# Forty products of zeros among the first four pairs of an attention and two-layer MLP kernel

## The chip, the cores and the metric

The kernel runs on one core of one Trainium2 chip. The metric is the device time of one execution in microseconds (us); of several executions the median counts. Before the change, three runs gave 1048.25, 1048.41 and 1051.59 us, so the median is 1048.41 us.

## The reference, cut to what matters

Causal attention over 4 batches, 8 heads, 576 positions of 64 channels, mixed with a read of a memory matrix, then two dense layers with a gate between their matrices, one after the other.

```python
scores = scale * np.matmul(q, k.transpose(0, 1, 3, 2))       # causal mask, softmax -> a
local = np.matmul(a, v)
mem_out = einsum('bhsd,bhde->bhse', phi(q), M_prev) / (einsum('bhsd,bhd->bhs', phi(q), z_prev) + 1e-6)
x = g * mem_out + (1 - g) * local                             # (2304, 512)
h = x @ w_in;  x = (h * sigmoid(1.702 * h)) @ w_out           # d_ff 2048
h = x @ w_in2; x = (h * clip(h + 3, 0, 6) / 6) @ w_out2
```

## The kernel before

The 2304 rows of x are cut into six tiles of 384 (`TILES`, a tile is one (batch, block) segment of 384 positions or two segments of 192). Attention works on one *pair* at a time: two heads of one segment; pairs 0 to 3 make tile 0. The generator `attention` runs three stages of a pipeline over pairs: in step i `scores(i)` issues the score products of pair i, `turn(i - 1)` the transposes of the softmax of the pair before, and `weigh(i - 2)` the products with v. `mem_read(i - 1)` issues the products with the memory matrix. The engines share a pair's work like this:

- PE (TensorE): score products `s` (line 424, by the helper `mm`), transposes `t` (line 439, `at_transpose`), memory products `mem` (line 409, `at_matmul`), and `o`, the transposed memory part and the products with v (line 424 again).
- DVE (VectorE): mask and row minimum of `s` (line 484), sums and reciprocals of `st` (lines 492 and 493), scaling of `mem` (lines 676 to 680), and `phi` (lines 654 and 655).
- ACT (ScalarE): the exponential `p` (line 489), the copies `pt` of the transposes out of PSUM (line 584), the copy of `o` into x (line 736).
- POOL (GpSimd): the norm of `p` (line 497).

PSUM has eight banks. While tile 0 is made, `bank` hands out all eight in turn (`banks[0] = 8`), so a product into a bank waits until the reader of what stood there has read it. After tile 0 the attention of tile t + 1 is mixed into the first dense layer of tile t: `h` (lines 342, and 344 to 347) and `y` (lines 313, and 315 to 317). The first tile's `h` and `y` multiply in full fp32, the rest in fp32r. The weights are made on DVE and ACT (lines 186 to 206) before that.

A scheduler places the instructions of each engine into one fixed order when the program is built, so an edit at one place can move instructions of other engines. At run time each engine takes its queue strictly in that order.

At the very start a tile `warm` of zeros is set by DVE, and PE multiplies it nine times with itself into a bank that nobody reads (`WARM = 9`).

Of the kernel before, what the change touches and what calls it, by code (L numbers as in the profile page):

```python
# [9 lines left out]
F32R = mybir.dt.float32r  # L10
# [12 lines left out]
NT = 384  # L23
# [27 lines left out]
AB = None  # L51
LAG = 3
WARM = 9
AHEAD = 2
TWB = (3, 2)
EARLY = 3
# [20 lines left out]
def f32(ap):  # L77
    return ap.bitcast(F32)
# [26 lines left out]
def attention_moe_kernel(ctx: ExitStack, tc: tile.TileContext, qk0, sk0, sk1, vm0, vm1, bb, w1, w2, out):  # L105
    nc = tc.nc
    PE, ACT, DVE, POOL, SP = nc.tensor, nc.scalar, nc.vector, nc.gpsimd, nc.sync
# [4 lines left out]
    gp = ctx.enter_context(tc.tile_pool(name="gp", bufs=2))  # L112
# [38 lines left out]
    def load_w(n):  # L151


        while w_at[0] < min(n, len(w_jobs)):
            key = layer, f = w_jobs[w_at[0]]
            w_at[0] += 1
            pool, tag = slot(layer, f)
            w_raw[key] = pool.tile([128, 2, 2 * DM], I32, tag=tag, bufs=1, name=f"r{f}")
            for a in range(2):
                move(0, out=w_raw[key][:, a], in_=(w1, w2)[layer][f, a].bitcast(I32))  # L160
# [7 lines left out]
    def conv_w():  # L168
# [7 lines left out]
        if layer == 0:  # L176
            load_w(min(NF, w_at[1] + AHEAD))
        z = 2 if layer == 1 else int(f > PRE)
# [203 lines left out]
    def bank(name):  # L382
        k = banks[1] % banks[0]
        banks[1] += 1
        if k < 3:
            t = psa.tile([128, 512], F32, tag="a", bufs=3, name=name)
            at = ("a", banks[2] % 3)
            banks[2] += 1
        else:
            tag = ("h", "y0", "y1", "y2", "y3")[k - 3]  # L390
            t = psy.tile([128, 512], F32, tag=tag, name=name)
            at = (tag, 0)
        place[id(t)] = at, t
        return t
# [10 lines left out]
    on_pe = []  # L405
    marks = [None]

    def at_matmul(out, **args):
        on_pe[:] = [PE.matmul(out, **args).ins]  # L409
# [28 lines left out]
    def at_transpose(*args):  # L438
        on_pe[:] = [PE.transpose(*args).ins]  # L439

    def attention(ap):
# [7 lines left out]
        def start(key, gen):  # L449
            gens[key] = chains.start(after_gates(gen, AB))  # L450

        def need(*keys):
            for key in keys:
                gen = gens.pop(key, None)
                if gen is not None:
                    chains.finish(gen)
# [122 lines left out]
        def evac(i, jobs):  # L579

            yield
            for e, out, in_, *bank_done in jobs:
                if e is ACT:
                    d = ACT.copy(out=out, in_=in_)
                else:
                    d = DVE.tensor_copy(out=out, in_=in_)
                made.setdefault(i, {})[e] = d.ins
                for t in bank_done:
                    has_read(t, d)

        def turn(i):
            ti, si, b, g, p, _ = pairs[i]
            if g == 0:
                pt[i] = []
                for a in range(2):
                    t = ap.tile([128, 2 * N0], F32, tag="pt", bufs=PTB, name="pt")
                    pt[i].append(t)
                    need(("s", i, 0), ("s", i, 1))
                    s = pp[i][a]
                    for jj in range(2):  # L600
                        ps = bank("t")
                        src = (((0, 0), (0, 128), (1, 0)), ((0, 256), (1, 128), (1, 256)))[jj]
                        for x, (y, c) in enumerate(src):
                            at_transpose(ps[:, x * 128:(x + 1) * 128], s[y][:, c:c + 128], ident)
                        start(("t", i, a, jj), evac(i, [((ACT, DVE)[EV0[jj]], t[:, jj * 384:(jj + 1) * 384], ps[:, 0:384], ps)]))
                        yield
            else:
                pt[i] = []
                for a in range(2):
                    t = ap.tile([128, 4, N1], F32, tag="pt", bufs=PTB, name="pt")  # L610
                    pt[i].append(t)
                    need(("s", i, 0))
                    ps = bank("t")
                    for j in range(4):
                        at_transpose(ps[:, j * 128:(j + 1) * 128], pp[i][a][0][:, j * 128:(j + 1) * 128], ident)
                    start(
                        ("t", i, a, 0),
                        evac(i, [((ACT, DVE)[EV1[a]], t[:, :, 0:128], ps.rearrange("p (j c) -> p j c", j=4), ps)]),
                    )
                    yield  # L620
                need(("s", i, 2))
                s, s5 = pp[i][2]
                ps = bank("t4a")
                for j in range(3):
                    at_transpose(ps[:, j * 128:(j + 1) * 128], s[:, j * 128:(j + 1) * 128], ident)
                ps2 = bank("t4b")
                at_transpose(ps2[:, 0:128], s[:, 384:512], ident)
                at_transpose(ps2[0:64, 128:256], s5, ident)
                v = ps[:, 0:384].rearrange("p (j a c) -> p j a c", j=3, a=2)
                start(  # L630
                    ("t", i, 0, 1),
                    evac(
                        i, [((ACT, DVE)[EV1[2 + a]], pt[i][a][:, 0:3, 128:192], v[:, :, a], *(ps,) * a) for a in range(2)]
                        + [(DVE, pt[i][a][:, 3, 128:192], ps2[:, a * 64:(a + 1) * 64]) for a in range(2)]
                        + [(DVE, t4[0:64], ps2[0:64, 128:256].rearrange("p (a c) -> p a c", a=2), ps2)]
                    ),
                )
                yield
            pp.pop(i)
# [117 lines left out]
        for i in range(NPAIR + 2):  # L757
            if has(i):
                gs[i] = scores(i)
            if has(i - 1):  # L760
                gt[i - 1] = turn(i - 1)
            if has(i - 2):
                gw[i - 2] = weigh(i - 2)
            s, t, w = gs.pop(i, nil), gt.pop(i - 1, nil), gw.pop(i - 2, nil)
            for gen, n in (
                (s, 1), (t, 1), (w, 1), (s, 1), (t, 1), (w, 9), (s, 1), (t, 1), (s, 9),
            ):
                yield from chunks(gen, n)
            if has(i):
                start(("p", i), mem_prep(i))  # L770
                load_qk(i + 2)
            if has(i - 2) and pairs[i - 2][5]:
                need(("x", i - 2))
                yield pairs[i - 2][0]
            load_vm(i)
            if has(i - 1):
                yield from mem_read(i - 1)
            yield from chunks(t, 9)


    with ExitStack():
        warm = gp.tile([128, 2, NT], F32R, tag="g", bufs=2, name="warm")
        DVE.memset(f32(warm[:, 0]), 0.0)
        s = bank("warm")
        for _ in range(WARM):
            PE.matmul(s[:, 0:NT], lhsT=warm[:, 0, 0:128], rhs=warm[:, 0], start=True, stop=True)
        ident = const.tile([128, 128], F32, name="ident")
        make_identity(nc, ident)
        mask = const.tile([128, 512], F32, name="mask")
# [169 lines left out]
```

## Time and profile before

| | |
|---|---|
| median of 3 runs | 1048.41 us |
| span of the profiled execution, taken as its own time | 1049.0 us |
| PE busy | 1029.6 us (98%) |
| DVE, ACT, POOL busy | 467.4, 510.2, 293.7 us |
| mean granted TensorE clock | 0.995 |

The profile shows one execution on the core. The clock is given as a share of 2.4 GHz: 1.00 is 2.4 GHz and 0.50 is 1.2 GHz. A row of the order-of-time view gives the start, the time from the first start to the last end of a run of alike instructions, the engine, the line, the operation, and in brackets the idle time ahead of it and what ended that. Ends of PE's products are modelled, starts are not. A product with full fp32 operands on 64 rows or with a fp32 result of several passes can be two records, so counts in the trace can be twice those of the program. The profiled execution's span stands 0.6 us over the median of the runs.

### The profile page before, as it was taken

What the parts mean: (1) busy time and instruction counts of PE and PEld (TensorE: products, weight loads), DVE (VectorE), ACT (ScalarE), POOL (GpSimd) and SP (SyncE); (2) the same over time, 40 slices, a digit from 0 to 9 for tenths busy, and PEclk for the clock granted to TensorE, in tenths of its full rate; (3) what the DMA queues carried; (4) which work ended last, traced back from release to release, by engine and by line L of the source; (5) the groups of instructions that cost most, each with busy time, mean ns of one, the idle gap of its engine ahead of it and who ended that gap; (6) DMA issues with size and microseconds to landing.
All of it is one profiled execution on the core that took longest, in us unless ns stands there. A gap on an engine that the chain in (4) does not pass through costs nothing.

```text
span 1049.0 us, 16113 instructions
## 1 busy us (share of the span) xinstructions
PE 1029.6 (98%) x6025; PEld 914.9 (87%) x6025; DVE 467.4 (45%) x1153; ACT 510.2 (49%) x1110; POOL 293.7 (28%) x346
## 2 busy tenths in 40 slices
PE   8899999999999999999999999999999999999998
PEld 5555558988888888898889999999999999999998
DVE  6977766666533343433443697971121211211110
ACT  5876746545634454433333778883232332332322
POOL 4522112333333332322222241332222222222221
PEclk8999999999999999999999999999999999999999
DMA  5864314332211021111100784001010010000000
GB/s 185 277 232 137 136 55 153 129 118 65 81 42 36 26 67 46 31 31 61 47 16 16 271 302 173 18 11 52 1 46 16 10 52 1 31 31 1 31 1 30
DMA packets 33885, 80.27 MB, mean 77 GB/s; under 512 B 4112, under 2 KB 13328, under 8 KB 33808
## 3 DMA queue, kind: packets, MB, share of 16 engines
q1 hardware_dynamic: 33808, 79.25, 22.4%
q8 instruction: 47, 0.77, 0.3%
q14 instruction: 30, 0.25, 0.1%
HBM read 61.41 MB, written 9.44 MB: 68 GB/s over the span
## 4 chain that ended last, share of the span: by engine, by line
PE 86%; DVE 6%; ACT 5%; issue 2%; DMA 1%; SPq 0%; POOL 0%; DVEq 0%; ACTq 0%
PE y L315 11%; PE h L344 11%; PE y L317 11%; PE y L316 11%; PE h L347 11%; PE h L346 11%; PE s L424 5%; PE o L424 5%; PE h L342 3%; PE y L313 3%; PE t L439 3%; ACT p L489 2%; PE mem L409 1%; DVE s L484 1%; DVE r L191 1%
## 5 line engine op out<-in xcount | busy, mean ns | idle before, releaser
L295 POOL TENSOR_TENSOR g<-t,g 128x384 fp32r<-128x384 f32 x173 | 185.2, 1071 | 481.6 <-ACT g L292 433.0
L344 PE MATMUL h<-xs,w 128*128 128x384 f32 x704 | 241.4, 343 | 1.6 <-DVE t L283 0.9
L315 PE MATMUL y<-g,w 128*128 128x384 f32 x704 | 237.2, 337 | 0.5 <-ACT g L292 0.5
L316 PE MATMUL y<-g,w 128*128 128x384 f32 x704 | 236.3, 336 | 0.0
L346 PE MATMUL h<-xs,w 128*128 128x384 f32 x704 | 236.0, 335 | 0.3 <-DVE w L228 0.3
L347 PE MATMUL h<-xs,w 128*128 128x384 f32 x704 | 236.0, 336 | 0.0
L317 PE MATMUL y<-g,w 128*128 128x384 f32 x704 | 223.6, 338 | 0.0
L287 DVE SCALAR_TENSOR_TENSOR t<-t,h 128x384 f32<-128x384 f32 x96 | 53.0, 553 | 275.5 <-ACT t L285 275.4
L344 PEld LDWEIGHTS h<-xs,w 128*128 128x128 f32 x704 | 132.3, 188 | 10.1 <-issue 5.2
L285 ACT ACTIVATE t<-h,three 128x384 f32<-128x384 f32 x96 | 55.6, 580 | 170.2 <-PE h L347 170.1
L497 POOL TENSOR_SCALAR p<-p,st,omg 128x128 f32<-128x128 f32 (+3 forms) x128 | 85.8, 683 | 186.3 <-DVE st L493 122.1
L317 PEld LDWEIGHTS y<-g,w 128*128 128x128 f32 x704 | 130.4, 188 | 5.6 <-issue 4.9
L315 PEld LDWEIGHTS y<-g,w 128*128 128x128 f32 x704 | 132.2, 188 | 2.8 <-issue 1.3
L292 ACT CAST g<-t 128x384 fp32r<-128x384 f32 x176 | 90.1, 514 | 90.9 <-DVE t L287 49.3
L346 PEld LDWEIGHTS h<-xs,w 128*128 128x128 f32 x704 | 132.4, 188 | 0.7 <-DVE w L228 0.5
L316 PEld LDWEIGHTS y<-g,w 128*128 128x128 f32 x704 | 132.2, 188 | 0.7 <-issue 0.5
L347 PEld LDWEIGHTS h<-xs,w 128*128 128x128 f32 x704 | 132.2, 188 | 0.5 <-issue 0.5
L489 ACT ACTIVATE p<-s,st 128x512 f32<-128x512 f32 (+4 forms) x160 | 82.5, 524 | 73.3 <-DVE st L484 61.5
L484 DVE CUSTOM_DVE_ANT_0 s<-s,mask 128x128 f32<-128x128 f32 (+3 forms) x144 | 72.3, 529 | 72.1 <-PE s L424 71.3
L281 ACT ACTIVATE t<-h 128x384 f32<-128x384 f32 x96 | 46.8, 491 | 66.8 <-PE h L347 54.7
L424 PE MATMUL s<-qk 64*128 64x256 f32 (+5 forms) x384 | 70.2, 461 | 3.3 <-ACT p L489 2.4
L283 DVE SCALAR_TENSOR_TENSOR t<-t,h 128x384 f32<-128x384 f32 x80 | 44.0, 552 | 62.5 <-ACT t L281 59.2
(82 smaller groups left out, 1111.9 us busy)
## 6 DMA issues: line engine op xcount, KB each, us to landing
r<-in_w_dram SPq DMA_DIRECT2D x64, 512.0 KB, 6.3
wt<-r SPq DMA_DIRECT2D x32, 256.0 KB, 2.3
vm<-in_vm_dram SPq DMA_DIRECT2D x16, 386.0 KB, 3.0
qk<-in_qk_dram SPq DMA_DIRECT2D x16, 384.0 KB, 3.5
qk<-in_sk_dram SPq DMA_DIRECT2D x32, 192.0 KB, 3.8
x2d<-yo SPq DMA_DIRECT2D x24, 192.0 KB, 2.0
xr<-x2d SPq DMA_DIRECT2D x24, 192.0 KB, 3.0
out_dram<-yo SPq DMA_DIRECT2D x24, 192.0 KB, 1.9
```

The lines of the kernel that those rows point to most:

```text
L292: gated["ACT"].append(ACT.copy(out=g[:, 0], in_=t).ins)
L295: d = {"DVE": DVE, "POOL": POOL}[e].tensor_tensor(out=g[:, 1], in0=t, in1=f32(g[:, 0]), op=ALU.subtract)
L315: PE.matmul(ys[d], lhsT=w[:, 0, o:o + 128], rhs=g[:, 0], start=(f == 0), stop=False)
L316: PE.matmul(ys[d], lhsT=w[:, 1, o:o + 128], rhs=g[:, 0], start=False, stop=False)
L317: PE.matmul(ys[d], lhsT=w[:, 0, o:o + 128], rhs=g[:, 1], start=False, stop=(f == NF - 1))
L344: PE.matmul(h, lhsT=w[:, 0, c:c + 128], rhs=x[:, 0], start=first, stop=False)
L346: PE.matmul(h, lhsT=w[:, 1, c:c + 128], rhs=x[:, 0], start=False, stop=False)
L347: PE.matmul(h, lhsT=w[:, 0, c:c + 128], rhs=x[:, 1], start=False, stop=last)
L424: ins = PE.matmul(out, **args).ins
L484: DVE.tensor_tensor_reduce(out=o, in0=o, in1=m, scale=-SCALE, scalar=init, op0=ALU.add, op1=ALU.min, accum_out=out)
L489: return ACT.activation(out=dst, in_=o, func=AF.Exp, scale=-1.0, bias=m, accum_out=s)
L497: (DVE, POOL)[e[norms[0] % len(e)]].tensor_scalar(out=dst, in0=dst, scalar1=s, scalar2=w, op0=ALU.mult, op1=ALU.mult)
```

## The change

For each of pairs 0 to 3, `turn` now issues ten more products ahead of the pair's first transpose, into the bank that this transpose will overwrite. They multiply `warm` (128 columns as weights) with 384, 512, 256 and 384 columns of `warm`. `tc.issue_after(on_pe[0])` asks the scheduler to place them behind the product that was emitted last. `warm` is laid out flat, and 512 of its columns are set to zero in place of 384. Nothing reads what these products write.

```diff
+FILL = ((10, 384), (10, 512), (10, 256), (10, 384))
...
                         ps = bank("t")
+                        if a == jj == 0 and i < len(FILL):
+                            count, n = FILL[i]
+                            with tc.issue_after(on_pe[0]):
+                                for _ in range(count):
+                                    at_matmul(ps[:, 0:n], lhsT=warm[:, 0:128], rhs=warm[:, 0:n], start=True, stop=True)
...
-        warm = gp.tile([128, 2, NT], F32R, tag="g", bufs=2, name="warm")
-        DVE.memset(f32(warm[:, 0]), 0.0)
+        warm = gp.tile([128, 2 * NT], F32R, tag="g", bufs=2, name="warm")
+        DVE.memset(f32(warm[:, 0:512]), 0.0)
...
-            PE.matmul(s[:, 0:NT], lhsT=warm[:, 0, 0:128], rhs=warm[:, 0], start=True, stop=True)
+            PE.matmul(s[:, 0:NT], lhsT=warm[:, 0:128], rhs=warm[:, 0:NT], start=True, stop=True)
```

The queues differ only in the first 60 or so rows of PE, 150 of DVE and 80 of ACT; behind these, buffer and line numbers aside, each engine's order is the same. POOL's is the same throughout. In the changed program the lines of `at_matmul`, `mm` and `at_transpose` are 410, 425 and 440.

The first place is PE's queue around the first transposes (pair 0's), before:

```order
L424 MATMUL s<-qk 128x128 x2
L424 MATMUL s<-qk 128x256 x2
L424 MATMUL s<-qk 128x384 x2
L439 MATMUL t<-ident,p 128x128 x4
L409 MATMUL mem<-vm,phi 128x130 x3
```

and of the change:

```order
L425 MATMUL s<-qk 128x128 x2
L425 MATMUL s<-qk 128x256 x2
L410 MATMUL t<-warm 128x384 x10
L425 MATMUL s<-qk 128x384
L440 MATMUL t<-ident,p 128x128
L440 MATMUL t<-ident,p 128x128 x8
L410 MATMUL mem<-vm,phi 128x130 x3
```

The ten products stand ahead of pair 1's 384-wide scores, and pair 0's memory products moved behind nine transposes. (The last 384-wide score product, left out here, stands between the first transpose and the other eight.)

The second place is PE's queue around pair 2's first scores and pair 0's `o`, before:

```order
L424 MATMUL s<-qk 128x128 x2
L424 MATMUL s<-qk 128x256 x2
L439 MATMUL t<-ident,p 128x128
L424 MATMUL o<-ident,mo 128x128 x3
L424 MATMUL o<-pt,vm 64x384 x2
L424 MATMUL o<-pt,vm 64x256 x2
L424 MATMUL o<-pt,vm 64x128 x2
L424 MATMUL s<-qk 128x384 x2
```

and of the change:

```order
L425 MATMUL s<-qk 128x128 x2
L425 MATMUL s<-qk 128x256 x2
L410 MATMUL t<-warm 128x512 x10
L440 MATMUL t<-ident,p 128x128 x6
L425 MATMUL o<-ident,mo 128x128 x3
L425 MATMUL o<-pt,vm 64x384 x2
L425 MATMUL o<-pt,vm 64x256 x2
L425 MATMUL o<-pt,vm 64x128 x2
L425 MATMUL s<-qk 128x384 x2
```

Ten products and six transposes of pair 1 now stand between pair 2's first scores and pair 0's `o`.

The third place is DVE's queue at pair 1's 384-wide minimum (`s_208` before, `s_218` of the change, first of two heads), before:

```order
L484 ISA s_208,st_162<-s_208,mask_93 128x384
L484 ISA st_162 128x1
L492 TENSOR_SCALAR st_162<-st_162 128x4
L493 RECIPROCAL st_162<-st_162 128x4
L484 ISA s_209,st_162<-s_209,mask_93 128x384
```

and of the change:

```order
L493 TENSOR_SCALAR st_162<-st_162 128x4
L494 RECIPROCAL st_162<-st_162 128x4
L485 ISA s_218,st_162<-s_218,mask_93 128x384
L485 ISA st_162 128x1
L485 ISA s_219,st_162<-s_219,mask_93 128x384
```

The first of the two 384-wide minima moved behind the sum and reciprocal of the narrower blocks.

## Rows read from the trace of the kernel before

**Rows 1.** The page's head: the span, and the engines' busy time, share, instructions
```profile
span 1049.0 us, 16113 instructions
PE 1029.6 (98%) x6025; PEld 914.9 (87%) x6025; DVE 467.4 (45%) x1153; ACT 510.2 (49%) x1110; POOL 293.7 (28%) x346
```

**Rows 2.** Busy us by stretch: length, PE, PEld, DVE, ACT, POOL, clock, DMA
```profile
7.90:10.30 2.40, 0.04 (x3) 0.00 (x1) 2.27 (x12) 0.97 (x5) 0.00 (x0) 1.00 1.03 405
10.50:17.20 6.70, 6.02 (x23) 3.95 (x21) 4.72 (x25) 4.87 (x21) 4.02 (x8) 0.50 0.37 119
17.70:36.60 18.90, 17.86 (x134) 11.44 (x133) 16.63 (x66) 16.45 (x54) 8.96 (x16) 1.00 0.51 183
36.60:51.90 15.30, 12.64 (x81) 7.38 (x80) 12.79 (x45) 11.74 (x32) 8.90 (x12) 1.00 0.98 319
...
140.50:143.70 3.20, 3.20 (x6) 1.69 (x6) 2.06 (x9) 1.45 (x4) 0.84 (x2) 0.52 0.00 0
```

**Rows 3.** The chain that ended last, from 9 to 55 us: start, us, what
```profile
9.33 1.73 ACT p L489 x8
...
51.86 2.85 PE h L342 x8
```

**Rows 4.** PE in order of time, from 1 to 38 us
```profile
1.31 3.25 PE L786 MATMUL warm<-warm 128*128 128x384 f32 x9 [1.31 <-DVE warm L783]
4.49 3.45 PE L424 MATMUL s<-qk 64*128 64x128 f32 x20
10.30 1.56 PE L424 MATMUL s<-qk 64*128 64x384 f32 x4 [2.36 <-ACT p L489]
...
17.73 0.93 PE L424 MATMUL s<-qk 64*128 64x128 f32 x8
...
18.95 0.55 PE L424 MATMUL o<-ident,mo 128*128 128x128 f32 x3
...
20.87 0.92 PE L424 MATMUL s<-qk 64*128 64x384 f32 x4
21.71 0.77 PE L439 MATMUL t<-ident,p 128*128 128x128 f32 x5
...
23.99 0.93 PE L424 MATMUL s<-qk 64*128 64x128 f32 x8 [0.40 <-ACT pt L584]
...
26.33 0.49 PE L424 MATMUL o<-ident,mo 128*128 128x128 f32 x3
...
28.20 0.88 PE L439 MATMUL t<-ident,p 128*128 128x128 f32 x6
28.91 0.83 PE L409 MATMUL mem<-vm,phi 128*128 128x130 f32 x6
...
31.51 0.33 PE L439 MATMUL t<-ident,p 128*128 128x128 f32 x1 [0.58 <-POOL p L497]
...
32.89 0.49 PE L424 MATMUL o<-ident,mo 128*128 128x128 f32 x3
...
37.55 0.33 PE L439 MATMUL t<-ident,p 128*128 128x128 f32 x1 [0.92 <-POOL p L497]
```

**Rows 5.** PE in order of time, 900 to 903 us, first and last of 20
```profile
899.67 0.33 PE L347 MATMUL h<-xs,w 128*128 128x384 f32 x1
...
902.96 0.33 PE L344 MATMUL h<-xs,w 128*128 128x384 f32 x1
```

**Rows 6.** ACT and DVE in order of time, from 14 to 23 us
```profile
14.72 0.60 DVE L484 CUSTOM_DVE_ANT_0 s<-s,mask 128x384 f32<-128x384 f32 x1
...
16.18 0.54 DVE L484 CUSTOM_DVE_ANT_0 s<-s,mask 128x384 f32<-128x384 f32 x1
...
16.28 0.49 ACT L584 COPY pt<-t 128x384 f32<-128x384 f32 x1
...
22.20 0.54 DVE L484 CUSTOM_DVE_ANT_0 s<-s,mask 128x384 f32<-128x384 f32 x1
```

**Rows 7.** PE in order of time, 112 to 142 us: the longest later idle time
```profile
140.16 2.29 PE L342 MATMUL h<-x,r 128*128 128x384 f32 x3 [2.46 <-DVE g L283]
```

## Prediction

> **What bounds the kernel now.** Start at the page's head: PE is busy for 98% of a span of 1049.0 us, DVE and ACT for under half [rows 1]. So a microsecond of PE work costs a microsecond wherever PE does not wait. The added products stand in the first 40 us, and there the share is another: look at the busy time by stretch. Four stretches matter [rows 2]. From 7.9 to 10.3 us PE is idle (0.04 of 2.40 us). From 10.5 to 17.2 us PE is busy for 6.02 of 6.70 us, but at a granted clock of 0.50, which is 1.2 GHz. From 17.7 to 36.6 us, pairs 1 to 3, the clock is 1.00 (2.4 GHz) and PE is busy for 17.86 of 18.90 us, so only 1.04 us is free. From 36.6 to 51.9 us it is busy for 12.64 of 15.30 us, 2.66 us free.
>
> Next, the chain that ended last [rows 3]: at 9.33 us it runs through ACT's exponentials, from 51.86 us through PE's `h`. So early on it is ACT (and DVE, between these rows) that it names, yet PE has just 1 us of room from 17.7 to 36.6 us: two limits lie side by side, and whichever is delayed becomes the one that counts.
>
> Last, PE in order of time [rows 4]. Before 10.30 us PE waits 2.36 us for an exponential of ACT: pair 1's 384-wide scores reuse the bank that this reads. What PE did before the clock fell was nothing, for those 2.36 us; what it did before the clock came back at about 17 us was some six busy microseconds.
>
> **Price of one product.** In the dense layers 20 starts of fp32r products of 384 columns lie between 899.67 and 902.96 us, 3.29 / 19 = 0.173 us from start to start at full clock [rows 5]. The nine products of zeros at the start took 3.25 us, 0.36 us each, which is the lower level's price [rows 4]. No row has 512 or 256 columns. In proportion they are 0.231 and 0.115 us; the 256-wide one may also stay at 0.173, if loading the weights sets the pace. So at full clock ten cost 1.73, 2.31, 1.15 to 1.73 and 1.73 us for pairs 0, 1, 2, 3.
>
> The page "TensorE: Matmul & The Clock Gate" of the Trainium skill, in "Back-to-back issue gap", gives N / 2.4 + 2.5 ns for a product of N columns at full clock. That would be 163 ns where the trace has 173, and by it, as an estimate, the last three sets are 4.9 us in all, so that the forecast below would be lower by some 0.6 us. The measurement decides.
>
> **Part by part.**
>
> *Zeroing 512 columns.* The first product waits 1.31 us, and with a third more columns it waits at most 0.44 us longer. That ends in the 2.36 us of idle time at 10.30 us [rows 4]: nothing. Without that cover it would be 0.44 us.
>
> *First ten.* The queue has them behind pair 1's first scores, which end at 4.49 + 3.45 = 7.94 us, in a bank that is still unused. The clock is 1.00 there, so they need 1.73 of the 2.36 us [rows 2, 4]: nothing. Uncovered they cost 1.73 us; at the lower level 3.6 us, 1.2 more than the gap. I expect the clock to stay at 2.4 GHz through 10 to 17 us. I value that at nothing: POOL norms for 4.02 of these 6.70 us [rows 2] and PE's transposes need the norms, and the chain stands with ACT there. The bounds are 0 and half of 6.02 us, -3.0 us.
>
> *Moved minimum.* DVE's first 384-wide minimum of pair 1 goes from 14.72 us to the place at 16.18 us [rows 6], behind a sum that waits for ACT. ACT's exponential and then its copy `pt`, which began at 16.28 us, follow some 1.1 us later, at 17.4 us, and take 0.5 us. Pair 2's first scores wait for this copy, since they get its bank: 17.9 us in place of 17.73 us, +0.2 us.
>
> *Second ten.* They stand behind these scores (0.9 us), and pair 0's `o` stands behind them and six transposes of pair 1 (28.91 - 28.20 = 0.71 us [rows 4]). So `o` starts at 17.9 + 0.9 + 2.3 + 0.7 = 21.8 us, not 18.95 us: +2.9 us. Pair 2's 384-wide scores, 1.92 us behind the start of `o`, go from 20.87 to 23.7 us and end 0.9 us later. The minimum that reads them began at 22.20 us [rows 6] and now begins at 24.6 us: DVE, and ACT behind it, are 2.4 us late. This is the step on which the forecast turns. Its cover is missing: PE had 1.22 us between the starts of those scores and of `o`, and spent 0.9 of them on the scores.
>
> *Third ten.* Between the `o` of pairs 0 and 1 lie 7.38 us (18.95 to 26.33). Of these 0.40 us were a wait, at 23.99 us [rows 4], and two transposes (0.2 us) have moved ahead. With 1.15 to 1.73 us added, the second `o` is 0.5 to 1.1 us later still: +3.4 to +4.0 us.
>
> *Last ten.* From 26.33 to 32.89 us the same sum gives +1.73, +0.24 for two transposes moved in, and up to -0.58 for the wait at 31.51 us [rows 4]: the third `o` is 4.8 to 6.0 us late, 5.2 us in the middle.
>
> *Where it is given back.* At 37.55 us PE waited 0.92 us for a norm of POOL [rows 4], and 2.66 us up to 51.9 us in all. If only PE were late, all of that would absorb delay. But DVE and ACT, for which PE waits, have been 2.4 us late since the second ten and are held up again by the last. I take 1.2 us as given back: the 0.9 us wait and a little of the rest. From 51.86 us on PE sets the end, and the queues are the old ones, so a shift stays.
>
> **Sum:** 5.2 - 1.2 = +4.0 us. From below: the three sets at their cheapest, 5.2 us, less all idle time, 1.04 + 2.66 us: +1.5 us. From above: at their dearest 5.8 us, with the 0.6 us that the moved minimum and transposes cost by themselves, and nothing given back: +6.4 us. Against the profiled execution this is 1049.0 + 4.0 = 1053.0 us. That execution stands 0.6 us over the median, so I forecast a median of **1052.4 us**, and 1049.9 to 1054.8 us for this case. About 0.3% (3.15 us) is what a measurement of this kernel tells from no change.
>
> **Rivals.**
>
> *The added products fit in* (1048.4 us, by 1.5 us either way). The busy time of products is modelled at its ends, and weight loads fill only 11.44 of 18.90 us in the stretch of pairs 1 to 3 [rows 2]. If loads measured the room, there would be 7.5 us of it, more than the 5.8 us that come in. "Perfetto Trace Analysis" of the Trainium skill, in "Identifying the Most-Contended Engine", says just this: judge TensorE's headroom by weight loading or useful work, not by the busy share of its products. Against it speak the starts, which are not modelled: `o` at 18.95, scores at 20.87, transposes at 21.71 us, one behind the other with no wait between [rows 4]. Chance 0.17.
>
> *Faster: PE did pace the slow stretch.* If it was PE's half clock from 10.5 to 17.2 us, rather than POOL and ACT, that held the start of pair 2, up to 3.0 us come back, and the waits that then open for `o` hide what is added. The later idle time of 2.46 us before 140.16 us [rows 7], behind which the clock is 0.52 for 3.2 us [rows 2], may also fall otherwise and spare 1.6 us. That gives -1.2 to -4.6 us, 1043.8 to 1047.2 us. It decides at pair 2's first scores: they must start well ahead of 17.7 us. Against it: they wait for the copy on ACT, which has moved back. Chance 0.19.
>
> *Slower: the clock falls all the same.* Behind the first ten, PE has only transposes and two score products to do until POOL's norms are through, so it may idle enough. Then the scores of pair 2 cost 0.9 us more and the second ten up to 4.8 rather than 2.3 us: +3.4 on top, +7.4 us, 1054.8 to 1057 us. Chance 0.12.
>
> That the products are dropped or placed elsewhere is excluded: all four sets stand in PE's queue.
>
> **How the numbers follow.** The forecast's case has 0.52. Above 1051.6 us, slower by over 0.3%, lie two thirds of it (0.35) and the last rival (0.12): slower 0.47. Below 1045.3 us lie most of the faster rival: 0.15. The rest, 0.38, is within 0.3%. The range from 1045.5 to 1056.0 us holds the forecast's case (alone 1049.9 to 1054.8 us), the first rival, and the nearer parts of the others.
>
> **What would show it.** Right: four runs of ten `t<-warm`, the first ending before 10.3 us; a clock of 1.00 from 10 to 17 us; pair 2's first scores at about 17.9 us; the three `o` near 21.8, 30 and 38 us; `h`, at 51.86 us before, near 56 us; the same queues and spacing after that. Wrong: scores of pair 2 before 17 us, or `o` within 1 us of 18.95 us, or `h` not later than before: then PE had room, or the clock was worth something.

## The result, and the profile after

The change is slower: the median of four executions is 1056.15 us (1055.55 to 1057.60), against 1048.54 us of four executions of the kernel before (1048.25 to 1051.59). The ratio is 1.0069, 95% interval 1.0055 to 1.0084, which is some 7.2 us. Two later groups of runs, below, repeat it at 1.0059 (1.0046 to 1.0071) and, with one transfer moved, at 1.0058. The direction was forecast; of the size, +4.0 us, the measurement shows more: 6 to 7 us by the three ratios.

The page's head of the change, and its busy us by stretch (columns as in [rows 2]):

```profile
span 1053.8 us, 16192 instructions
PE 1035.0 (98%) x6065; PEld 920.5 (87%) x6065; DVE 467.8 (44%) x1153; ACT 510.5 (48%) x1110; POOL 293.1 (28%) x346
...
7.90:10.30 2.40, 1.88 (x8) 0.95 (x6) 1.87 (x9) 1.91 (x9) 0.00 (x0) 1.00 1.00 380
11.80:15.00 3.20, 3.20 (x12) 2.12 (x12) 2.09 (x11) 1.72 (x8) 2.14 (x4) 0.50 0.29 81
...
17.70:36.60 18.90, 18.90 (x132) 13.58 (x130) 14.38 (x62) 14.08 (x42) 9.59 (x14) 1.00 0.51 182
```

PE's busy time is 5.4 us more, the span 4.8 us more [rows 1]. The idle stretch ahead of 10.30 us has been filled for the most part (1.88 of 2.40 us busy, before 0.04). From 17.7 to 36.6 us nothing is left of the 1.04 us that were free [rows 2]: PE is busy for 18.90 of 18.90 us. The clock is at 0.50 from 11.8 to 15.0 us, where before it was there from 10.5 to 17.2 us.

PE in order of time after the change; the first rows answer to [rows 4], the last one to [rows 7]:

```profile
6.86 2.01 PE L410 MATMUL t<-warm 128*128 128x384 f32 x10
9.36 0.91 PE L425 MATMUL s<-qk 64*128 64x384 f32 x2 [0.48 <-ACT p L490]
...
17.02 0.93 PE L425 MATMUL s<-qk 64*128 64x128 f32 x8 [0.99 <-ACT pt L585]
17.88 2.60 PE L410 MATMUL t<-warm 128*128 128x512 f32 x10
20.31 0.82 PE L440 MATMUL t<-ident,p 128*128 128x128 f32 x6
20.96 0.49 PE L425 MATMUL o<-ident,mo 128*128 128x128 f32 x3
...
26.01 1.46 PE L410 MATMUL t<-warm 128*128 128x256 f32 x10
27.31 0.38 PE L440 MATMUL t<-ident,p 128*128 128x128 f32 x2
...
28.74 0.49 PE L425 MATMUL o<-ident,mo 128*128 128x128 f32 x3
...
33.88 2.01 PE L410 MATMUL t<-warm 128*128 128x384 f32 x10
35.72 0.82 PE L440 MATMUL t<-ident,p 128*128 128x128 f32 x6
...
37.31 0.55 PE L425 MATMUL o<-ident,mo 128*128 128x128 f32 x3
...
47.34 0.94 PE L410 MATMUL mem<-vm,phi 128*128 128x130 f32 x6 [1.92 <-ACT p L490]
...
48.65 2.85 PE L343 MATMUL h<-x,r 128*128 128x384 f32 x8
52.47 0.93 PE L425 MATMUL s<-qk 64*128 64x128 f32 x8 [0.97 <-DVE mo L686]
...
54.45 0.55 PE L425 MATMUL o<-ident,mo 128*128 128x128 f32 x3 [0.57 <-ACT pt L585]
...
56.44 2.85 PE L343 MATMUL h<-x,r 128*128 128x384 f32 x8
...
144.94 4.45 PE L343 MATMUL h<-x,r 128*128 128x384 f32 x8 [2.46 <-DVE g L284]
```

From the start of a set to the start of the transposes behind it, the last three sets take 2.43, 1.30 and 1.84 us, 5.57 us together. That is 0.184 us for one of 384 columns, where the dense layers have 0.173 [rows 5]. No row from 17.88 to the fourth `o` at 42.79 us carries a wait.

Ahead of comparing starts one thing has to be taken out. The chain of each kernel begins with the same transfer, which lands at 6.56 us before and at 5.61 us after (first the row of before, then that of the change):

```profile
1.65 4.91 DMA qk<-in_qk_dram
```

```profile
1.64 3.97 DMA qk<-in_qk_dram
```

Its landing differs from execution to execution and shifts all that follows. So the starts below count from ACT's second `phi`, which waits for this transfer (6.58 and 5.64 us). The fourth `o`, the first and second `h` of before and PE's waits between them are these rows:

```profile
39.93 0.49 PE L424 MATMUL o<-ident,mo 128*128 128x128 f32 x3
...
43.78 0.55 PE L439 MATMUL t<-ident,p 128*128 128x128 f32 x3 [0.39 <-ACT p L489]
44.53 2.85 PE L342 MATMUL h<-x,r 128*128 128x384 f32 x8 [0.20 <-ACT pt L584]
...
49.68 0.55 PE L424 MATMUL o<-ident,mo 128*128 128x128 f32 x3 [0.97 <-ACT pt L584]
...
51.86 2.85 PE L342 MATMUL h<-x,r 128*128 128x384 f32 x8 [0.18 <-DVE g L283]
```

The `h` behind 2.46 us in the last column is the one of [rows 7].

| us from the second `phi` to the start of | first `o` | second | third | fourth | first `h` | second `h` | `h` behind 2.46 us |
|---|---|---|---|---|---|---|---|
| before | 12.37 | 19.75 | 26.31 | 33.35 | 37.95 | 45.28 | 133.58 |
| the change | 15.32 | 23.10 | 31.67 | 37.15 | 43.01 | 50.80 | 139.30 |
| difference | +2.95 | +3.35 | +5.36 | +3.80 | +5.06 | +5.52 | +5.72 |
| no products (below) | 12.36 | 19.75 | 26.32 | 33.36 | 37.97 | 45.29 | 133.86 |
| the change again (below) | 15.32 | 23.10 | 31.67 | 37.14 | 43.00 | 50.79 | 139.31 |

Two executions of one queue agree to 0.02 us in the first six columns, so the differences up to 51 us belong to the queues and not to the execution. The loss is there by the second `h` and stays: +5.75 us at the end of the span (4.8 us, and 0.95 us for the earlier transfer).

The chain that ended last, of the change, now passes through the second set, where before it named ACT and DVE (compare [rows 3]):

```profile
17.95 2.53 PE t L410 x10
...
44.18 6.55 DMA qk<-in_sk_dram
```

The transfer in its last row lands at 50.73 us. The instruction behind it in the chain, ACT's `r`, starts at 50.71 us, right after DVE's `r` that it reads (49.11 + 1.56 us). So that this transfer held anything up is not shown.

### The profile page after: what moved, and what is told of

Same layout as the page of the kernel before. It is cut to its first block, busy times and chain, and to the rows that moved or that the text cites. A ratio compares the mean times of both kernels' runs of the same rounds, so it can differ in the third digit from the quotient of the medians.

```text
span 1053.8 us, 16192 instructions
## 1 busy us (share of the span) xinstructions
PE 1035.0 (98%) x6065; PEld 920.5 (87%) x6065; DVE 467.8 (44%) x1153; ACT 510.5 (48%) x1110; POOL 293.1 (28%) x346
## 4 chain that ended last, share of the span: by engine, by line
PE 83%; DVE 6%; ACT 6%; issue 2%; DMA 2%; SPq 0%; POOL 0%; DVEq 0%; ACTq 0%; POOLq 0%
PE y L316 11%; PE y L317 11%; PE y L318 11%; PE h L345 10%; PE h L347 10%; PE h L348 10%; PE o L425 5%; PE s L425 5%; PE h L343 3%; PE y L314 3%; PE t L440 3%; ACT p L490 2%; DVE r L192 1%; PE mem L410 1%; ACT r L196 1%
## 5 line engine op out<-in xcount | busy, mean ns | idle before, releaser
L345 PEld LDWEIGHTS h<-xs,w 128*128 128x128 f32 x704 | 132.3, 188 | 10.2 <-issue 5.2
```

The source lines that it names most:

```text
L345: PE.matmul(h, lhsT=w[:, 0, c:c + 128], rhs=x[:, 0], start=first, stop=False)
```

## Experiments: the first set alone, the others alone, twice as many

Theory A says that the change costs what the sets in TensorE's unbroken stretch cost in time. Theory B says that the order, which the scheduler moved along with them, costs it. The first expectations call A the PE-time theory and B the order theory; the clock theory is that a shorter stretch at the lower clock is worth something. The first four kernels have all sets empty, the first alone, the last three, and twenty products in each:

```diff
-FILL = ((10, 384), (10, 512), (10, 256), (10, 384))
+FILL = ((0, 384), (0, 512), (0, 256), (0, 384))
+FILL = ((10, 384),)
+FILL = ((0, 384), (10, 512), (10, 256), (10, 384))
+FILL = ((20, 384), (20, 512), (20, 256), (20, 384))
```

No products:

> No products added, only 512 columns of the tile set to zero; PE's queue is that of before. PE-time theory, order theory and clock theory alike: within 0.1% of before (1048.5 us, 1047.5 to 1049.5). It serves as the profile to compare the others with: a clock of 0.50 somewhere in 10 to 17 us, the three o near 18.9, 26.3 and 32.9 us.

Measured: 1051.40 us, ratio to before 1.0010 (0.9998 to 1.0022). Before itself is at 1050.08 us in this group, so the ratio counts: it lies at the edge of the 0.1% expected. Zeroing 512 columns and laying out `warm` flat costs nothing that can be told apart, and the table shows the same starts.

The first set alone:

> Only pair 0's ten products. PE-time theory (the cost is the PE time of the later three sets, 5.6 us in the trace of the change, where PE has no room): within 1 us of before, since these ten lie in PE's wait for ACT. Order theory (the moved DVE and ACT instructions cost by themselves, most of them around pair 1, and these moves are here too): +3 us or more. Clock theory (the shorter stretch at 1.2 GHz is worth something): 1 to 3 us faster than before.

Measured: 1051.57 us, ratio 1.0013 (1.0003 to 1.0023), some 1.4 us. That is nearest to the PE-time theory's 1 us; the order theory's 3 us and the clock theory's gain lie outside the interval. Its PE in order of time:

```profile
7.82 2.01 PE L410 MATMUL t<-warm 128*128 128x384 f32 x10
10.30 0.91 PE L425 MATMUL s<-qk 64*128 64x384 f32 x2 [0.47 <-ACT p L490]
...
19.80 0.66 PE L440 MATMUL t<-ident,p 128*128 128x128 f32 x4 [0.82 <-POOL p L498]
20.29 0.49 PE L425 MATMUL o<-ident,mo 128*128 128x128 f32 x3
```

The ten lie in the wait and the scores behind them start at 10.30 us, as they did before. But the moved order puts four transposes that wait for POOL ahead of the first `o`: counted from `phi` it starts at 13.72 us (+1.35), and the second `h` at 47.42 us (+2.1). So order has a price of its own. That the median shows less of it goes with a higher mean clock of these executions (below).

The last three sets:

> The change without pair 0's ten. PE-time theory: as the change, +6 to +8 us on before. Order theory: less than the change by the moves around pair 1's minimum that are not here, +2 to +5 us. Clock theory: slower than the change by 1 us or more, since the clock falls earlier and for longer.

Measured: 1055.85 us, ratio 1.0049 (1.0032 to 1.0067); 4.5 us over the run without products. That lies between the ranges of the PE-time and the order theory and decides nothing between them; slower than the change, as the clock theory had it, it is not. The fourth `o` starts at 36.51 us from `phi`, +3.16 us over before where the change has +3.80: so most of the loss is there without the first ten. The second `h` starts at 50.94 us from `phi`, 0.14 us from the change's 50.80, though in this execution the first `o` was only 1.46 us late (13.83 us), and a wait of 2.40 us for `vm` and a fall of the clock came in behind the fourth. So the two agree at the second `h` by chance.

Twenty in each:

> Twenty products in place of ten in each of the four sets. PE-time theory: the later three sets take 5.6 us more and the first overruns its gap by about 1.3 us, so +12 to +15 us on before (1060.5 to 1063.5 us). Order theory: about as the change, +5 to +9 us. Clock theory: at most as the change, since PE is busier in the early stretch, +7 us or less.

Measured: 1057.82 us, ratio 1.0072 (1.0056 to 1.0088). The first `o` starts at 18.11 us (+5.7), the `h` behind the long wait at 143.43 us (+9.9). That is less than twice the change's +5.72, and the median, +7.7 us, gives less still: the PE-time theory's +12 to +15 us is missed, and the order theory's +5 to +9 us holds it. The stretch up to the fourth `o` says otherwise. There the last three sets take 4.67, 2.49 and 3.58 us, 5.2 us more than in the change, and the four `o` start at 18.11, 26.30, 36.90 and 42.46 us, the fourth 5.3 us later than in the change. So the added products cost their own time there. Behind it this run wins back 1.6 us on the change up to the second `h` (54.51 us), and behind the long wait its clock stays at 1.00, which is worth 1.7 us (`h` 2.85 us, below). The order is another one here, so the run is no clean doubling.

## Experiments: the second set made thin

In both of these TensorE's queue and VectorE's are in the order of the change:

```diff
-FILL = ((10, 384), (10, 512), (10, 256), (10, 384))
+FILL = ((10, 384), (10, 8), (10, 256), (10, 384))
+FILL = ((10, 384), (1, 512), (10, 256), (10, 384))
```

Ten products of 8 columns, and the change itself on the same chip:

> The second set's ten products are 8 columns wide instead of 512; every engine's order is that of the change. Theory A (what the change costs is the time that TensorE spends on the sets that lie in its unbroken stretch): the second set shrinks from 2.43 us start to start to an estimated 1.1 to 1.3 us, so the run is 1.1 to 1.3 us faster than the change of the same job, and the first `o` starts about that much earlier after the second transfer of qk landed. Theory B (the moved order of the queues is what costs, the products run beside it): the same time as the change, within 0.3 us. Both: the first 10 to 17 us look as in the change.

> The change itself, on the chip of these runs, to pair the others with. Theory A and theory B alike: 5 to 7.5 us slower than before, as it was the first time.

Measured: the change 1055.66 us, ratio 1.0059 (1.0046 to 1.0071), as expected; with the thin set 1057.88 us, ratio 1.0080 (1.0067 to 1.0092). The thin set makes it slower still, which neither theory expected. PE in order of time and the clock of the stretch tell why:

```profile
17.40 1.65 PE L425 MATMUL s<-qk 64*128 64x128 f32 x8 [0.61 <-ACT pt L585]
18.98 2.29 PE L410 MATMUL t<-warm 128*128 128x8 f32 x10
21.14 1.54 PE L440 MATMUL t<-ident,p 128*128 128x128 f32 x6
22.47 0.85 PE L425 MATMUL o<-ident,mo 128*128 128x128 f32 x3
```

```profile
14.40:24.60 10.20, 9.59 (x43) 7.40 (x45) 4.78 (x24) 6.70 (x24) 5.19 (x10) 0.50 0.09 32
```

The clock fell at about 14.4 us and stayed at 0.50 up to 24.6 us, past the set. At that level ten 8-wide products take 2.16 us (18.98 to 21.14), hardly less than ten 512-wide ones at full clock (2.43 us), and the scores, transposes and `o` around them take about twice as long. All five executions had a mean clock of 0.993, of the change's nine only one. The run tells nothing between A and B; it shows what the lower clock costs where PE has no room: the first `o` at 16.45 us from `phi`, 1.13 us behind the change.

One product of 512 columns keeps the set short without a row of narrow ones:

> The second set is one product 512 columns wide instead of ten (wide, so that no long row of narrow products runs); TensorE's and VectorE's orders are those of the change, two instructions of ScalarE change places. Theory A (the sets cost their own time): 2.43 us become about 0.24, so 2.2 us faster than the change, about +4.0 us on before (ratio 1.0038), and the first `o` starts some 13.1 us after the second transfer of qk landed, where the change had 15.3. Theory B (the moved order costs): as the change, 1.0059 to 1.0069.

Measured: 1054.76 us, ratio 1.0045 (1.0029 to 1.0062). The interval holds theory A's 1.0038 and the lower end of theory B's range, so the median does not decide; the starts do. Its PE in order of time:

```profile
17.88 0.51 PE L410 MATMUL t<-warm 128*128 128x512 f32 x1
...
18.84 0.66 PE L440 MATMUL t<-ident,p 128*128 128x128 f32 x4 [0.23 <-POOL p L498]
19.33 0.49 PE L425 MATMUL o<-ident,mo 128*128 128x128 f32 x3
...
46.33 1.64 PE L410 MATMUL mem<-vm,phi 128*128 128x130 f32 x6 [2.52 <-ACT p L490]
...
48.40 3.39 PE L343 MATMUL h<-x,r 128*128 128x384 f32 x8
```

Counted from `phi`, all four `o` start 1.6 us ahead of the change's (13.72, 21.50, 30.07, 35.56 us): with TensorE's order untouched, the nine products are worth 1.6 us there, not the 2.2 us of theory A, since a wait for POOL opens in their place. The first `o` is still 1.35 us later than before: this rest is not the second set's own time but that of the moved order. At `mem` 1.0 us of the 1.6 is left, since PE waits 2.52 us for ACT's `p` where the change waits 1.92 us. At the second `h` it is 0.7 us (50.08 against 50.80), but in this execution the clock fell in that wait (`mem` 1.64 us for 0.94, `h` 3.39 for 2.85), which adds 1.2 us to these two rows. So up to the fourth `o` theory A holds for most of the loss and theory B for the rest; behind it PE waits for other engines.

## Experiments: the last set alone, and one transfer

The last set alone, where TensorE's order stays close to that of before:

```diff
-FILL = ((10, 384), (10, 512), (10, 256), (10, 384))
+FILL = ((0, 8), (0, 8), (0, 8), (10, 384))
```

> Only the last set, ten products 384 wide ahead of the fourth pair's transposes; TensorE's order is otherwise nearly that of before. Theory A: the ten take 1.84 us start to start and the transposes behind them lose a wait of 0.58 us, so about 1.3 us slower than before, and `h` that began at 51.86 us begins about 1.3 us later, counted from the landing of qk's second transfer. Theory B: order hardly moves, so 0 to 0.4 us slower.

Measured: 1054.39 us, ratio 1.0049 (1.0035 to 1.0062). Ten products that took 1.84 us in the change cost 4.5 us, more than either theory expected. The chain and PE in order of time:

```profile
36.60 11.44 DMA vm<-in_vm_dram
```

```profile
48.18 1.64 PE L410 MATMUL mem<-vm,phi 128*128 128x130 f32 x6 [5.72 <-DMA vm<-in_vm_dram]
...
50.25 4.80 PE L343 MATMUL h<-x,r 128*128 128x384 f32 x8
```

Up to there the price is small: the third `o` is 1.1 us late and the fourth 0.6 us (33.93 us from `phi`). Then PE waits 5.72 us for the fifth pair's `vm`. The scheduler has moved this transfer behind four weight transfers `r` in SP's queue, and it lands 11.44 us after its issue (before: 3.4 us). The list of changed queues ahead of the prediction leaves out SP's, which the change moves too. The clock falls in the wait, and `h` takes 4.80 us in place of 2.85. In the change three of the four `r` stand ahead of it. So two more kernels force it ahead of the four, in the run just told and in the change, with all other engines' orders as they were:

```diff
+            if i == 4:
+                fifth.append(d.ins)
...
+            with tc.issue_after(fifth[0]) if key in ((0, 3), (0, 4)) else ExitStack():
                 for a in range(2):
                     move(0, out=w_raw[key][:, a], in_=(w1, w2)[layer][f, a].bitcast(I32))
...
+                with tc.issue_after(fifth[0]) if fifth else ExitStack():
                     move(4, out=x[a], in_=wx[f][:, a])
```

> As the run with the last set alone, but with the fifth pair's vm transfer issued ahead of the four transfers of r, as in before; all engines' orders stay. Theory E (that run was slow because vm came late behind r): the wait of 5.72 us ahead of `mem` goes, and the time falls from +4.5 us to the set's own +1.3 to +2 us on before (ratio 1.001 to 1.002). Rival: another wait takes its place (the next transfer of qk, or ScalarE's p), and less than 1 us is gained (1.004 or more).

Measured: 1051.71 us, ratio 1.0013 (1.0001 to 1.0025), as theory E had it. Of PE's rows:

```profile
44.39 0.94 PE L415 MATMUL mem<-vm,phi 128*128 128x130 f32 x6 [1.32 <-ACT p L497]
```

The wait for `vm` is gone. A wait of 1.32 us for ACT's `p` stands there, where before waited 0.39 us for `p`, right behind `mem`; the second `h` is 2.4 us late in this trace. From +4.5 to +1.4 us over before: some 3 us were the place of one transfer in SP's queue and what it brought with it, not TensorE's work.

> The change, with the same transfer put ahead of those of r. Theory A: there it landed at about the time at which ScalarE's p let TensorE go on anyway, so within 0.5 us of the change (ratio 1.0055 to 1.007). Theory E, if it holds for the change too: 1.5 us or more faster than the change (1.0045 or less).

Measured: 1055.77 us, ratio 1.0058 (1.0043 to 1.0073), and the second `h` at 50.81 us from `phi`, the change's 50.80. In the change the transfer's place costs nothing. It is issued at the same time either way (33.7 us from `phi`) and lands 7.7 us later in the change and 3.1 us later here, and in both PE goes on only when ACT's `p` lets it.

## Experiments: can products in idle time gain?

If the clock's falls cost time, zeros in TensorE's idle time might give some back. One kernel puts two fp32 products into the wait of 2.46 us [rows 7], the other adds four products of the first set, which hardly move the order:

```diff
+            if exact and f == 13:
+                mm = in_a_run([phase["tanh"]])
+                for _ in range(2):
+                    mm(ys[3], lhsT=ident, rhs=mask[:, 0:NT], start=False, stop=False)
...
+FILL = ((4, 384),)
```

> None of the forty products; instead two fp32 products by zeros, 384 columns wide, added into the accumulator of the second block just before the last `h` of the first row tile, in TensorE's wait of 2.46 us near 140 us. Theory C (the clock's drop behind that wait costs time: h takes 4.5 us there instead of 2.85): the granted clock stays at 1.00 behind it, and the run is 0.5 to 1.6 us faster than before, depending on how many executions dropped there. Theory D (that drop is made up for later, or falls at another place): within 0.3 us of before.

Measured: 1049.15 us, ratio 0.9996 (0.9987 to 1.0005). PE in order of time, and the clock of two stretches:

```profile
139.20 1.56 PE L428 MATMUL y<-mask,ident 128*128 128x384 f32 x4 [1.07 <-ACT t L281]
140.62 2.85 PE L346 MATMUL h<-x,r 128*128 128x384 f32 x8
```

```profile
10.40:20.60 10.20, 8.96 (x36) 5.86 (x36) 8.03 (x35) 6.63 (x26) 6.09 (x12) 0.50 0.18 64
140.60:143.40 2.80, 2.80 (x10) 1.72 (x10) 2.42 (x9) 1.45 (x4) 0.08 (x1) 1.00 0.00 0
```

Before has this row there:

```profile
140.16 4.51 PE L342 MATMUL h<-x,r 128*128 128x384 f32 x8 [2.46 <-DVE g L283]
```

The clock stays at 1.00 behind the wait and `h` takes 2.85 us in place of 4.51 us, in the other kernel's trace too. So a fall there costs 1.7 us. That the two products prevent it is likely but not shown: of the twelve traces without them, nine have the fall, and three (the last three sets, twenty in each, the last set alone) have an `h` of 2.85 us behind the same wait. In the execution with the two products the lower clock at the start lasted to 20.6 us, past the first `o`, and cost 0.8 us there; the products stand 120 us behind it and cannot have caused that. The interval reaches from 1.4 us faster to 0.5 us slower than before, so a gain of theory C's lower size is neither found nor excluded.

> Meant to beat both: four products 384 wide ahead of the first pair's transposes, where TensorE's order stays nearly that of before, and the two fp32 products near 140 us. Theory C (the stretches at the lower clock cost time and products in idle time shorten them): more executions with a mean clock of 0.998, 1 to 2 us faster than before (ratio 0.998 to 0.999). Theory D: within 0.3 us of before.

Measured: 1050.43 us, ratio 1.0005 (0.9994 to 1.0016): not faster, and theory C's 1 to 2 us are outside the interval. Without a fall from 10.5 to 16 us, its profile has one behind that (a granted clock of 0.63 from 16.2 to 20.8 us), and the first `o` is 1.2 us late. No version tried was measured faster than the kernel before.

The mean granted clock of every execution of before shows what the falls go with. In 59 executions the span is 1046.1 to 1047.9 us at a mean clock of 0.998 (23 of them), 1048.0 to 1050.3 at 0.995 (12), 1049.1 to 1050.1 at 0.993 (11). So the falls of the clock go with up to 3 us. The change's nine executions have 0.993 to 0.997, none has 0.998. At equal clock it is 5.3 to 6.5 us slower (0.995: 1054.0 against 1048.7 us in the mean; 0.997: 1054.8 against 1048.3 us). The first set alone ran at a mean of 0.9971, before at 0.9960: at 0.998 its span was 1049.0 to 1049.4 us, 2.3 us over that of before, about what its trace shows at the second `h` (+2.1). So a higher mean clock seems to offset part of the price of the order; no run separates the two.

## Why the prediction was right in direction and short in size

*Price and places.* Sets at 2.43, 1.30 and 1.84 us make 5.57 us, within the 5.2 to 5.8 forecast. The estimate from the formula on the page "TensorE: Matmul & The Clock Gate" of the Trainium skill, in "Back-to-back issue gap", was 4.9 us; the trace disagrees by 0.7 us. This page of the Trainium skill gives the formula for a single product by itself; for a stream of products that each load their weights it has about 131 ns at 512 columns, where the trace has 243 ns. The measurement decides.

*First ten and zeroing.* The zeroing costs nothing, as forecast, and the ten fit into the wait, as forecast. But the run with the first set alone shows a price of the order that they move: 1.35 us at the first `o`, 2.1 us at the second `h`, of which its median shows some 1.4 us. The forecast has the nine products at the start at the lower level; the profile has 1.00 granted from 1.3 to 4.5 us, so that level is not shown there.

*Moved minimum, second, third and last ten.* Counted from `phi`, pair 2's first scores are 0.2 us late (forecast 0.2), the three `o` 2.95, 3.35 and 5.36 us (forecast 2.9, 3.4 to 4.0, 5.2). These steps were right to 0.2 us. (The middle of the forecast's 4.8 to 6.0 us is 5.4 rather than 5.2 us, and its sum then +4.2 us.) From pair 2's first scores to the first `o` PE now works without a wait, as summed: 0.86 us of scores, 2.43 us of the set, 0.65 us of transposes. How much of the delay is the sets' own time, the single 512-wide product shows: 1.6 us on all four `o`, at TensorE's order. The other 1.35 us at the first `o` remain with the moved order, because a wait for POOL opens where the nine products were.

*Where it is given back.* This is the step that failed. The forecast took 1.2 us off, for the 0.92 us wait at 37.55 us, and let the rest stand from 51.86 us on. At the fourth `o` 1.56 us had in fact come back (+5.36 to +3.80). But 1.72 us were lost again up to the second `h` (+5.52). That is just what PE's waits between these two grew by: 3.46 us after the change (1.92 on ACT's `p` ahead of `mem`, 0.97 on DVE's `mo`, 0.57 on ACT's `pt`), 1.74 us before (0.39, 0.20, 0.97 and 0.18 us). ACT's first exponential and first 384-wide exponential of the fifth pair, before and after, show where it grows:

```profile
39.85 0.37 ACT L489 ACTIVATE p<-s,st 128x128 f32<-128x128 f32 x1 [0.74 <-DVE st L484]
41.73 0.58 ACT L489 ACTIVATE p<-s,st 128x384 f32<-128x384 f32 x1
```

```profile
44.21 0.37 ACT L490 ACTIVATE p<-s,st 128x128 f32<-128x128 f32 x1 [2.20 <-DVE st L485]
46.59 0.61 ACT L490 ACTIVATE p<-s,st 128x384 f32<-128x384 f32 x1
```

Counted from `phi`, the pair's scores start 4.15 us late on PE (37.80 and 41.01 us), the first of these exponentials 5.30 us late and the second 5.80 us. In the change DVE takes a `phi` and the other head's 128-wide minimum ahead of the 256-wide one, and ACT takes the copies `x` and `pt` ahead of the first 384-wide exponential; before, they stood behind it. I held the queues of DVE and ACT to be merely late; they also do their work in another order there. Lateness alone need not cost this: with twenty in each, later still, only 0.1 us was lost between the fourth `o` and the second `h`, and TensorE's order there has `h` ahead of `mem`. With a single set and `vm` in its old place it was 0.8 us. The net of the step is +0.2 us rather than -1.2 us, and the sum +5.7 us in the trace rather than +4.0 us. Which of the moved instructions costs how much, no run isolates.

The profiled execution of before was taken to stand 0.6 us over the median, its span being read as its time. In every execution on record the time is 1.7 to 3.8 us longer than the span, so it stands further above. The forecast adds +4.0 us to the median either way, so its number does not change.

*The clock.* I expected 2.4 GHz from 10 to 17 us and valued it at nothing. It fell all the same, at 11.8 us, and came back at 15.0 us. In the traces its value there is small: before has 0.50 for 6.7 us, the run without products for some 3.3 us, and their first `o` start within 0.01 us of each other. But where it lasted past 20 us it cost 0.8 to 1.1 us at the first `o`, and over executions, the falls go with up to 3 us, a spread between executions that the forecast did not have. That the change never shows 0.998, while before often does, would account for ratios that stand for 6 to 7 us where two traces, at 0.995 and 0.996, differ by 5.7; this is argued from the lists of clocks, and no run tests it.

*The rivals.* "Fit in" fell: PE is busy for 18.90 of 18.90 us, though weight loads fill only 13.58 of them. By the Trainium skill's page "Perfetto Trace Analysis", in "Identifying the Most-Contended Engine", more than a quarter would still be free; here no wait was left to use. "Faster" was to decide at pair 2's first scores, and they came no sooner. "The clock falls all the same" holds the measured time in its range, but not its mechanism: the clock was back at 1.00 ahead of the second ten, which took 2.43 us and not 4.8.

## What to carry to other kernels

Judge the room for added work by the waits in the stretch where it is put, and count starts from an event that all executions share; then a queue's price shows to a few hundredths of a microsecond. Where a scheduler lays out the queues, look at every queue that an edit moves, the transfers' too: one `vm` behind four weight loads cost about twice what the ten products ahead of it did. Work put in to hold the clock has to lie in idle time and leave the order alone. And before a trace without a fall is credited to an edit, look whether traces without the edit have it every time: here three of twelve had none.

## What was not expected of the hardware

- The landing of one transfer of 384 KB at the start varied from 5.36 to 6.69 us among the profiled executions, and moved all behind it.
- With ten products of 8 columns in the second set the granted clock was 0.50 for 10.2 us, with ten of 512 columns in the same place it was 1.00 from 15 us on. A stretch of the same length occurred once without narrow products, so that they cause it is likely but not shown.
- Four executions of one queue had mean clocks from 0.993 to 0.996 and spans from 1053.8 to 1055.8 us, and those of before differ by up to 4.8 us, with the same queues.
